# Five unread bfloat16 products of zeros ahead of each unit's and each chunk's work on TensorE, in a graph tensor product

## The chip, the cores and the metric

The kernel runs on one core of a Trainium2 chip. The metric is the device time of one execution in microseconds (us). Three runs of the kernel before took 8650.16, 8655.81 and 8651.81 us; the median is 8651.81 us.

## The reference, cut to what matters

There are N = 10000 nodes and E = 640000 edges; C = 64 channels and M = 4 components, so one node's features are 256 floats.

```python
def reference(x, src, dst, Y, edge_feat, w_rad, cg, w_mix):
    R = _silu(edge_feat @ w_rad)                              # (E, C)
    xs = x[src]                                               # (E, C, M)
    tp = jnp.einsum('eci,ef,ifo->eco', xs, Y, cg)             # (E, C, M)
    msg = R[:, :, None] * tp
    agg = _segment_sum(msg.reshape(-1, C * M), dst, N).reshape(N, C, M)
    return jnp.einsum('ncm,cd->ndm', agg, w_mix)
```

## The kernel before

The kernel sorts the edges by their destination on the chip, gathers each edge's source features from HBM, and adds up the messages of each bucket of 32 nodes with matrix products. The edges come in three parts (30, 35.5 and 34.5 per cent).

**First pass.** It takes chunks of 12 tiles of 128 edges and sorts them into 18 groups of nodes. `spread` (VectorE, DVE: X at L572) lays each edge's nine words into slots, `rows` (DVE L588; ScalarE, ACT: L594 and L595) makes a one-hot matrix oh, `move` (TensorE, PE: L602) multiplies the two into a PSUM tile pr, `evict` (ACT, L609) copies pr to rt, and `store` (GpSimd, POOL: L613) scatters rt to HBM with an indirect DMA. The tile pr has two buffers, X and oh three each; both passes share them.

**Second pass.** The same code (`route`) sorts a group into buckets, in chunks of 11 tiles, with one further product at L604 where a row is carried over from the chunk before. Ahead of the chunks, small tables are worked out on PE, DVE and ACT (L365 to L508; L365 is a series of bfloat16 products that count, L463 to L471 make destinations).

**Units.** `messages` handles one bucket of one part at a time: 939 units, 5 tiles in part 0 and 6 in the others. For unit k: `gather` (POOL, L893) issues one indirect DMA a tile, five units ahead, into one of 7 buffers xg. `turn` (PE, L911, two products) transposes the edge words into PSUM tile pre (two buffers), `turned` (ACT, L916) copies them out, `radial` (PE, L923 and L924) makes the radial factors in the same pre, `silu` (ACT, L927) applies the function. `spots` (DVE, L935 and L938) makes S. `products` (DVE, L945) multiplies the gathered features in place by the radial factors; it is the last reader of pre. `sums` (PE, L958) adds the unit up in one half of the PSUM tile G, with 10 or 12 float32 products that the profile shows as 20 or 24 records, and is the last reader of xg. `evict` takes that half of G out: by ACT in part 0 (L989), by DVE in parts 1 and 2 (L987), where the sum so far comes back from HBM. In part 2 `mix` (PE, L1006) multiplies four buckets' sums by the weights, and the result is stored.

**Order.** The first pass of part 0 runs alone (lag = 2). All the rest, called the main phase here, is one program with lag = 1, in which `groups` interleaves the units, the first pass of parts 1 and 2 and the second pass by counted steps. On PE, DVE and ACT the order of the main phase is the order of the code, and an engine executes it in order; POOL's and SP's order is chosen by the scheduler. One step of `messages` has four quarters:

```python
quarters = (((index, LI), (gather, LG), (fetch, 2), (turn, 2), (sums, 0), (silu, 1)), ((turned, 2), (spots, 1)),
            ((products, 1), (evict, -1), (pieces, 4)), ((radial, 2), (full, -1)))
```

The number beside a stage is the unit's distance, so in step k PE gets turn(k + 2) and then sums(k), and at the end radial(k + 2); DVE gets products(k + 1) and behind it evict(k - 1). turn(k + 2) takes the buffer of pre that products(k) read last, and sums(k) takes the half of G that evict(k - 2) read last.

After the last unit, two short loops treat rows that did not fit (L1123 to L1199).

Of the kernel before, what the change touches and what calls it, by code (L numbers as in the profile page):

```python
# [19 lines left out]
BF = mybir.dt.bfloat16  # L20
# [5 lines left out]
P = 128  # L26
# [10 lines left out]
LG = 5  # L37
LI = 8
HEAVY = 4
BIG = 16384.0  # L40
FAR = 2097152.0
KR = 108
# [31 lines left out]
class Kernel:  # L74
    def __init__(self, ctx, tc, x, src, dst, Y, ef, w_rad, cg, w_mix, out):
# [58 lines left out]
        self.tab = {}  # L134
        self.held, self.wanted, self.pos = None, False, None

    def bank(self, key):

        while self.held or self.wanted:
            yield "held"  # L140
        self.held = key


    def consts(self):
        nc, c = self.nc, self.cst

        def iota(name, pat, base=0, cm=0, at=c):
            t = at.tile([P] + [n for _, n in pat], F, name=name)
            nc.gpsimd.iota(t, pattern=pat, base=base, channel_multiplier=cm,
                           allow_small_or_imprecise_dtypes=True)  # L150
            return t

        self.zr = c.tile([16, max(self.p1.rw, self.p2.rw)], F, name="zr")
        nc.vector.memset(self.zr, 0.0)
        self.pid = iota("pid", [[0, 1]], cm=1)
        self.pid1 = iota("pid1", [[0, 1]], base=1, cm=1)
        self.i128 = iota("i128", [[1, P]])

        self.dv = self.ps.tile([P, 512], F, name="dv", tag="dv", bufs=1)
        self.v128 = self.dv[:, 0:P]  # L160
        nc.vector.tensor_copy(self.v128, self.i128)
        self.i32 = self.dv[:, 0:NB]
        self.eq = self.dv[:, P:P + UT * NB].rearrange("p (t n) -> p t n", n=NB)
        self.vmsk = self.dv[:, P + UT * NB:-B // 2]

        ib = self.ph.tile([P, B], BF, name="ib", bufs=1)
        nc.vector.tensor_copy(ib, self.i128[:, :B])
        nc.vector.tensor_copy(self.dv[:, -B // 2:].bitcast(I32), ib.bitcast(I32))
        self.vb = self.dv[:, -B // 2:].bitcast(BF)
        d = iota("dif", [[1, P]], cm=-1, at=self.ph)  # L170
        self.ident = c.tile([P, P], F, name="ident")
        nc.vector.tensor_scalar(self.ident, d, 0.0, None, op0=OP.is_equal)
        self.U = c.tile([P, P], F, name="U")
        nc.vector.tensor_scalar(self.U, d, 0.5, None, op0=OP.is_ge)

        self.U2 = c.tile([32, 2, 32], F, name="U2")
        self.id2 = c.tile([64, 32], BF, name="id2")
        for h in range(2):
            nc.vector.tensor_copy(self.U2[:, h, :], self.U[:32, :32])
            nc.vector.tensor_copy(self.id2[32 * h:32 * h + 32, :], self.ident[:32, :32])  # L180
        for p in (self.p1, self.p2):

            p.on = c.tile([64, B * (p.T + 1)], F, name="on" + p.key)
            nc.vector.memset(p.on, 1.0)
            nc.vector.memset(p.on.rearrange("p (b t) -> p b t", b=B)[:, :, 0:1], 0.0)
            p.cols = c.tile([64, B * (p.T + 1)], F, name="cols" + p.key)
            nc.vector.memset(p.cols, 0.0)
        self.Ub = c.tile([P, P], BF, name="Ub")
        nc.vector.tensor_copy(self.Ub, self.U)
        self.A = c.tile([P, P], BF, name="A")  # L190
        nc.vector.scalar_tensor_tensor(self.A, self.ident, BIG, self.U, op0=OP.mult, op1=OP.add)
        self.ones = c.tile([P, P], F, name="ones")
        nc.vector.memset(self.ones, 1.0)
        self.onesb = c.tile([P, P], BF, name="onesb")
        nc.vector.memset(self.onesb, 1.0)
        self.sel = c.tile([P, 2 * P], BF, name="sel")
        nc.vector.memset(self.sel, 0.0)
        nc.vector.memset(self.sel[:, P:P + 1], 1.0)
        nc.vector.memset(self.sel[:, P + 32:P + 33], 1.0)

        self.gb, self.gc = [], []
        for k in range(len(SPLIT)):
            gb = iota("gb%d" % k, [[self.p1.stride, B]], base=k * self.NG * self.p1.stride)
            gc = c.tile([P, B], F, name="gc%d" % k)
            nc.vector.memset(gc, 0.0)
            for g in range(self.NG):
                nc.vector.memset(gb[:, g:g + 1], float(self.gbase[k][g]))
                nc.vector.memset(gc[:, g:g + 1], float(self.gt[k][g] * P // self.p1.r))
            self.gb.append(gb)
            self.gc.append(gc)  # L210

        self.k1 = c.tile([1, B], F, name="k1")
        self.k2 = c.tile([1, self.NG * B], F, name="k2")
        self.kov = c.tile([1, 2], F, name="kov")
        nc.vector.memset(self.k2, 0.0)
        nc.vector.memset(self.kov, 0.0)
        self.bb = iota("bb", [[self.p2.stride, B]])
        self.bn = iota("bn", [[NB, B]])
        self.bc = c.tile([P, B], F, name="bc")
        nc.vector.memset(self.bc, float(self.p2.cap))  # L220
# [291 lines left out]
    def route(self, ps, quad, nt, table):  # L512
# [4 lines left out]
        nc, wk, tc, T, Q = self.nc, self.ph, self.tc, ps.T, 2  # L517
# [20 lines left out]
        def placed(q):  # L538
            m = min(Q * T, nt - q * Q * T)
            pp = PS.pop(q)  # L540
            pc = PP[q] = wk.tile([P, Q * T, B], F, name="pc", tag="pc" + ps.key, bufs=1)
            nc.scalar.activation(pc[:, :m, :], pp[:, :m, :], AF.Copy, bias=-BIG)  # L542

# [54 lines left out]
        def move(c):  # L598
            X, oh, m, on = XO.pop(c)
            pr = self.ps.tile([P, 512], F, name="pr", tag="route", bufs=2)  # L600
            for u in range(m):
                nc.tensor.matmul(pr[:, :ps.rw], oh[:, u, :], X[:, u, :], start=(u == 0), stop=(not on and u == m - 1))  # L602
            if on:
                nc.tensor.matmul(pr[:, :ps.rw], oh[:, m, :], RT[c - 1], start=False, stop=True)  # L604
            PR[c] = pr
# [17 lines left out]
        for k in range(-3 * Q, N + self.ls):  # L623
            if 0 <= k - lag - 1 < N:
                evict(k - lag - 1)
            if 0 <= k - lag < N:
                move(k - lag)
            if k % 2 and 0 <= k + 5 < N:

                while self.pos:  # L630
                    yield "held"
                self.pos = ps.key
                places((k + 5) // 2)
            if k % 2 == 0 and 0 <= k + 4 < N:
                placed((k + 4) // 2)
                self.pos = None
            if k % 2 == 0 and 0 <= k + 6 < N:
                prepare((k + 6) // 2)
            if 0 <= k < N:
                spread(k)  # L640
                yield "half"
                rows(k)
            if k % 2 and 0 <= k + 3 < N:
                slots((k + 3) // 2)
            if 0 <= k - self.ls < N:
                store(k - self.ls)

            yield (HEAVY - 2 if k < N else HEAVY) if 0 <= k < N + lag else 1

# [176 lines left out]
    def pass2_steps(self, k, g):  # L826
        nch = (self.gt[k][g] + self.p2.T - 1) // self.p2.T

        return 2 * (8 + self.ls) + HEAVY * nch + 20 * ((k, g) == self.segs[k * self.NG])


    def messages(self):

        nc, ph = self.nc, self.ph
        units = [((k, g), j, s) for k, g in self.segs for j in range(self.nb(g)) for s in range(len(SPLIT[k][1]))]
        MT = max(sum(u) for _, u in SPLIT)
        n = len(units)
# [172 lines left out]
        def mixed(k, po):  # L1010
# [5 lines left out]

        Gb, self.turns = self.ps.tile([P, 2, 2, NB, 4], F, name="G", tag="G", bufs=1), 0

        quarters = (((index, LI), (gather, LG), (fetch, 2), (turn, 2), (sums, 0), (silu, 1)), ((turned, 2), (spots, 1)),
                    ((products, 1), (evict, -1), (pieces, 4)), ((radial, 2), (full, -1)))  # L1020
        todo, po = [], None
        for k in range(-LI, n + 3):
# [16 lines left out]
    def groups(self):  # L1039
# [13 lines left out]
        for k in range(1, len(SPLIT)):  # L1053
            end = max(ends[k * NG - 2] - 8, at + 1)
            n = self.chunks(k)
            later.append((self.pass1(k, self.p1.NC), at, end, HEAVY * n + 20 * (n / (self.p1.NC - 2) + 2)))
            at = end
# [212 lines left out]
```

## Time and profile before

The profiled execution has a span of 8660.7 us from the first to the last instruction, 8.9 us above the median of the runs; no other time is shown for it.

| | busy us | instructions |
|---|---|---|
| PE, products | 6942.9 | 52148 |
| DVE | 7173.7 | 13741 |
| ACT | 4089.0 | 11736 |
| POOL | 6041.3 | 6308 |

The mean granted clock of TensorE over the span is 0.894 of full speed. A busy figure counts an engine's instructions alone; a product's record reaches from its start to its end, and since products follow one another in a pipeline their durations overlap. "X <- Y: a, b, c" in the view of waits says that X stood idle until Y released it, a us in total, b times, c us at the longest.

### The profile page before, as it was taken

How to read it: one execution, taken by the hardware profiler on the slowest of the kernel's cores; microseconds unless marked ns; L12 is line 12 of the kernel's file. 1: busy time of each engine (PE TensorE's matmuls, PEld its weight loads, DVE VectorE, ACT ScalarE, POOL GpSimd, SP SyncE). 2: the span in 40 equal slices, each digit the busy share in tenths (PEclk: the TensorE clock that was granted, in tenths of full speed). 3: DMA queues.
4: the chain of work that ended last, by engine and by line, in shares of the span. 5: the costliest groups of instructions: out<-in, count | busy, mean ns of one | idle time of the engine just before them, and what ended most of it. 6: DMA issues, size and time to landing. Idle time of an engine off the chain costs nothing. (4 is left out here: it accounts for less than half of the span.)

```text
span 8660.7 us, 149335 instructions
## 1 busy us (share of the span) xinstructions
PE 6942.9 (80%) x52148; PEld 6380.0 (74%) x52148; DVE 7173.7 (83%) x13741; ACT 4089.0 (47%) x11736; POOL 6041.3 (70%) x6308
## 2 busy tenths in 40 slices
PE   7978888888888778888888888866888878788875
PEld 6867777777777677777777777766777767777764
DVE  8989899889998788999989998877877768677754
ACT  6866555555556455454544554433333323333310
POOL 1236777667777767777777777777777777777775
PEclk9989999889999889999889899888998889888887
DMA  9313434334433434444444444444444444444442
GB/s 169 104 58 99 123 115 119 103 113 117 121 110 111 122 106 132 135 132 138 133 130 136 135 133 134 128 138 132 128 125 125 125 124 124 122 128 125 124 123 83
DMA packets 696289, 1056.64 MB, mean 122 GB/s; under 512 B 252018, under 2 KB 500226, under 8 KB 695536
## 3 DMA queue, kind: packets, MB, share of 16 engines
q0 software_dynamic: 286560, 746.71, 30.3%
q1 hardware_dynamic: 406384, 292.76, 12.2%
q8 instruction: 412, 6.75, 0.3%
q10 hardware_dynamic: 2592, 7.63, 0.3%
q14 instruction: 341, 2.79, 0.1%
HBM read 856.08 MB, written 207.12 MB: 123 GB/s over the span
## 5 line engine op out<-in xcount | busy, mean ns | idle before, releaser
L893 POOL DMA_INDIRECT xg<-in_x_dram,sidx x5321 | 5067.8, 952 | 1739.3 <-issue 1386.5
L602 PE MATMUL pr<-X,oh 128*128 128x126 f32 (+1 forms) x21112 | 2765.2, 289 | 395.7 <-ACT rt L609 215.6
L958 PE MATMUL G<-S,xg 128*128 128x128 f32 x21284 | 2953.1, 302 | 98.1 <-DVE Gp L987 62.8
L602 PEld LDWEIGHTS pr<-X,oh 128*128 128x128 f32 x21112 | 2638.2, 201 | 477.8 <-ACT rt L609 264.2
L958 PEld LDWEIGHTS G<-S,xg 128*128 128x128 f32 x21284 | 2803.5, 215 | 139.3 <-DVE Gp L987 86.2
L945 DVE TENSOR_TENSOR xg<-xg,pre 128x1536 f32<-128x1536 f32 (+1 forms) x939 | 1556.8, 1658 | 710.5 <-DMA xg<-in_x_dram,sidx 586.4
L594 ACT ACTIVATE sq<-i,rowf 128x128 f32<-128x128 f32 x5605 | 1735.7, 393 | 13.9 <-DVE rowf L559 13.4
L572 DVE TENSOR_TENSOR X<-dv,Wt 128x1512 f32<-128x1512 f32 (+4 forms) x958 | 1588.4, 1658 | 149.0 <-PE pr L602 94.8
L927 ACT ACTIVATE pre<-pre 128x384 f32<-128x384 f32 (+1 forms) x939 | 430.8, 459 | 1694.7 <-PE pre L924 1204.7
L595 ACT ACTIVATE oh<-sq,ones 128x768 f32<-128x768 f32 (+3 forms) x958 | 932.1, 973 | 32.9 <-issue 5.5
L938 DVE TENSOR_TENSOR S<-dv,pay 128x768 f32<-128x768 f32 (+1 forms) x939 | 857.4, 913 | 48.0 <-PE G L958 2.8
L613 POOL DMA_INDIRECT grp<-rt,idx x417 | 415.5, 996 | 585.9 <-ACT rt L609 240.1
L588 DVE TENSOR_TENSOR oh<-dv,rowf 128x640 f32<-128x640 f32 (+2 forms) x922 | 792.2, 864 | 0.5
L613 POOL DMA_INDIRECT bkt<-rt,idx x541 | 543.2, 1004 | 221.7 <-issue 125.8
L911 PE MATMUL pre<-identb,e 128*108 128x128 bf16 x1878 | 277.3, 231 | 523.4 <-DVE xg L945 513.6
L911 PEld LDWEIGHTS <-e 128*108 128x108 bf16 x1878 | 219.9, 133 | 604.5 <-issue 515.2
L916 ACT ACTIVATE sT<-pre 108x256 bf16<-108x256 f32 x939 | 353.5, 376 | 631.1 <-PE pre L911 628.4
L1006 PE MATMUL po<-wf,Gs 128*128 128x256 f32 (+2 forms) x1392 | 382.3, 436 | 150.7 <-DVE Gs L987 150.5
L542 ACT ACTIVATE pc<-pp 128x432 f32<-128x432 f32 (+3 forms) x506 | 243.7, 482 | 524.1 <-DVE pos L551 407.3
L1006 PEld LDWEIGHTS po<-wf,Gs 128*128 128x128 f32 (+2 forms) x1392 | 277.5, 205 | 238.3 <-DVE Gs L987 166.8
L609 ACT ACTIVATE rt<-pr 128x135 f32<-128x135 f32 (+1 forms) x958 | 258.8, 273 | 269.4 <-DMA bkt<-rt,idx 181.4
L923 PE MATMUL pre<-wr,sT 108*128 108x192 bf16 x939 | 240.2, 256 | 142.2 <-ACT sT L916 141.8
(240 smaller groups left out, 5309.3 us busy)
## 6 DMA issues: line engine op xcount, KB each, us to landing
xg<-in_x_dram,sidx POOLq DMA_INDIRECT x5321
sums<-Gp SPq DMA_DIRECT2D x626, 128.0 KB
old<-sums SPq DMA_DIRECT2D x626, 128.0 KB
bkt<-z SPq DMA_DIRECT2D x24, 994.5 KB
pay<-bkt SPq DMA_DIRECT2D x34, 486.0 KB
ys<-in_Y_dram SPq DMA_DIRECT2D x104, 96.0 KB
es<-in_edge_feat_dram SPq DMA_DIRECT2D x104, 96.0 KB
out_dram<-ot SPq DMA_DIRECT2D x69, 128.0 KB
```

The lines of the kernel that those rows point to most:

```text
L572: nc.vector.tensor_tensor(X[:, :m, :].rearrange("p t (s w) -> p t s w", w=W), msk.unsqueeze(3).to_broadcast([P, m, ps.r, W]), QD[c // Q][1 ...
L588: nc.vector.tensor_tensor(oh[:, :v, :], self.v128.unsqueeze(1).to_broadcast([P, v, P]), row[:, o:o + v].unsqueeze(2).to_broadcast([P, v, P ...
L594: nc.scalar.activation(sq[:, u, :], self.i128, AF.Square, bias=to, scale=-1.0)
L595: nc.scalar.activation(oh[:, v:v + len(at), :], sq[:, :len(at), :], AF.Relu, bias=self.ones[:, 0:1], scale=-2.0)
L602: nc.tensor.matmul(pr[:, :ps.rw], oh[:, u, :], X[:, u, :], start=(u == 0), stop=(not on and u == m - 1))
L613: st = nc.gpsimd.indirect_dma_start(out=ps.dst, out_offset=bass.IndirectOffsetOnAxis(ap=idx[:, i:i + 1], axis=0), in_=RT.pop(c), in_offset ...
L893: nc.gpsimd.indirect_dma_start(out=xg[:, t, :], out_offset=None, in_=self.x, in_offset=bass.IndirectOffsetOnAxis(ap=si[:, u:u + 1], axis=0))
L911: nc.tensor.matmul(pre[:KR, 256 + 128 * h:384 + 128 * h], e[:, 36 * t:36 * t + KR], self.identb, start=True, stop=True)
L938: nc.vector.tensor_tensor(S[:, :ut], self.eq[:, :ut].unsqueeze(3).to_broadcast([P, ut, NB, 4]), pb[:, :, 1:5].unsqueeze(2).to_broadcast([P ...
L945: nc.vector.tensor_tensor(V, V, R.unsqueeze(3).to_broadcast([P, ut, 64, 4]), op=OP.mult)
L958: nc.tensor.matmul(G[:, h].rearrange("p n f -> p (n f)"), V[:, t, 32 * h:32 * h + 32, :].rearrange("p c i -> p (c i)"), S[:, t].rearrange( ...
L1006: nc.tensor.matmul(po[:nn, :256], Gs[:, h, f].rearrange("p b n -> p (b n)")[:, :nn], self.wf[:, h, f, :], start=(h + f == 0), stop=(h + f ...
```

## The change

A helper `keep` issues n products of a bfloat16 tile of zeros zb: 128 columns of it are the weights and 256 the moving operand. The main phase calls it with n = 5 at two places. In `move`, ahead of a chunk's products, the result goes to columns 256 to 511 of the chunk's own pr tile, of which the chunk uses at most 135 of the first columns. In `messages`, a new stage `busy` ahead of `turn` writes to the half of G that this step's `sums` is about to start afresh. Nothing reads the results of either.

```diff
+KEEP = 5
@@ Kernel
+    def keep(self, out, n):
+
+        for _ in range(n):
+            self.nc.tensor.matmul(out, self.zb[:, :P], self.zb, start=True, stop=True, skip_group_check=True)
@@ consts
+        self.zb = c.tile([P, 256], BF, name="zb")
+        nc.vector.memset(self.zb, 0.0)
@@ move
             pr = self.ps.tile([P, 512], F, name="pr", tag="route", bufs=2)
+            if self.lag == 1:
+                self.keep(pr[:, 256:], KEEP)
             for u in range(m):
@@ messages
-        quarters = (((index, LI), (gather, LG), (fetch, 2), (turn, 2), (sums, 0), (silu, 1)), ((turned, 2), (spots, 1)),
+        def busy(k):
+            self.keep(Gb[:, self.turns % 2].rearrange("p h n f -> p (h n f)"), KEEP)
+
+        quarters = (((index, LI), (gather, LG), (fetch, 2), (busy, 0), (turn, 2), (sums, 0), (silu, 1)), ((turned, 2), (spots, 1)),
```

## The prediction

> **What bounds the kernel now.** I read the page first, then the busy time by stage, then the waits of each stage. The stages are A (800 to 3200 us) and B (3200 to 5600), in which units, first-pass and second-pass chunks are mixed, and C (5600 to 8450), in which the first pass is over; these three rows give length, then busy us and count of PE, weight loads, DVE, ACT and POOL, then the granted clock.
>
> ```profile
> span 8660.7 us, 149335 instructions
> ...
> 800.00:3200.00 2400.00, 1955.75 (x15302) 1819.66 (x15301) 2147.47 (x4165) 1341.98 (x3928) 1717.31 (x1787) 0.91 0.40 114
> 3200.00:5600.00 2400.00, 1968.16 (x15328) 1834.56 (x15327) 2170.00 (x3996) 1205.60 (x3428) 1815.90 (x1891) 0.91 0.46 133
> 5600.00:8450.00 2850.00, 2262.54 (x16132) 2063.49 (x16131) 2071.41 (x3745) 972.67 (x2686) 2161.71 (x2259) 0.88 0.44 126
> ```
>
> POOL's 70% misleads. Between two gathers stands a pause of 0.3 us that nothing explains but "issue" (1240 such pauses in stage A, below, of 0.3 at the longest), so a POOL instruction takes 1717.31 / 1787 = 0.96 us and the pause. With 0.3 us on each instruction POOL is taken for 1717 + 1787 x 0.3 = 2253 of 2400 us in A, 1816 + 567 = 2383 of 2400 in B, and 2162 + 678 = 2840 of 2850 in C. In B and C POOL is full; in A it stands idle for some 147 us. DVE stands at 89% and 90% in A and B and at 73% in C; PE at 81%, 82% and 79%.
>
> The waits of stage A (of POOL, of PE, of DVE), then the longest of DVE and one of POOL in B, and the longest of DVE in C:
>
> ```profile
> POOL xg L893 <- issue: 377.8, 1240, 0.3
> POOL xg L893 <- PE G L958: 81.0, 42, 7.7
> ...
> POOL xg L893 <- PE stp L451: 15.3, 3, 13.2
> POOL xg L893 <- PE pre L924: 14.5, 16, 4.6
> POOL xg L893 <- PE pre L911: 13.1, 18, 4.1
> ```
> ```profile
> PE pre L911 <- DVE xg L945: 147.1, 73, 6.8
> PE pr L602 <- ACT rt L609: 112.9, 78, 4.3
> PE ddp L469 <- DVE to L463: 47.0, 15, 8.1
> PE pr L602 <- DVE oh L588: 25.8, 21, 4.9
> ```
> ```profile
> DVE X L572 <- PE pr L602: 48.7, 23, 5.4
> DVE sts L471 <- PE ddp L469: 25.8, 13, 5.5
> ...
> DVE xg L945 <- ACT pre L927: 13.1, 12, 2.5
> ```
> ```profile
> DVE Gp L987 <- PE G L958: 34.4, 20, 5.8
> DVE X L572 <- PE pr L602: 33.9, 16, 6.6
> ```
> ```profile
> POOL xg L893 <- PE G L958: 10.1, 12, 3.5
> ```
> ```profile
> DVE xg L945 <- DMA xg<-in_x_dram,sidx: 507.2, 135, 6.8
> ```
>
> In A, POOL waits for PE to free gather buffers: 81.0 + 15.3 + 14.5 + 13.1 = 123.9 us, or 100 without the 79 pauses of 0.3. There the loop of DVE, PE and ACT sets the pace, with DVE its busiest member. In B neither side holds the other: POOL waits 10.1 us for sums, and DVE's two longest waits, 34.4 and 33.9 us, are for PE, so that what it waits for gathered data is less; both go at almost the same pace. In C DVE waits 507 us for data: POOL sets the pace alone, and the others have room. A gain is thus capped at about 100 + 10 us, and a loss in A, and in most of B, goes into the time.
>
> **What the change adds.** 939 groups of five on G and 834 on pr (958 chunks less the 124 that part 0 has under lag = 2), 8865 products, each with a weight load, and one memset. Nothing is removed; the waits move. For a product's price the nearest rows are the bfloat16 counting products in a row, at full clock and, in C, at half:
>
> ```profile
> 4456.11 1.08 PE L365 MATMUL cnt<-D,sel 128*64 128x198 bf16 x11
> ```
> ```profile
> 6535.56 1.88 PE L365 MATMUL cnt<-D,sel 128*64 128x198 bf16 x11
> ```
>
> Eleven take 1.08 us; leaving some 0.19 for the last one to run out, a step is about 0.089, and (1.88 - 0.23) / 10 = 0.165 at half clock. The loads are hidden in that. For 256 columns in place of 198 this is 0.115 and 0.213, so five cost 0.57 us at full and 1.07 at half clock. Lower bound of a group: nothing, where PE would have idled; upper bound 1.07.
>
> The clock matters because PE loses it after its own waits:
>
> ```profile
> 4003.07 2.90 PE L958 MATMUL G<-S,xg 128*128 128x128 f32 x24
> ...
> 4008.10 1.74 DVE L945 TENSOR_TENSOR xg<-xg,pre 128x1536 f32<-128x1536 f32 x1
> ...
> 4009.76 0.41 DVE L987 TENSOR_TENSOR Gp<-old,G 128x256 f32<-128x256 f32 x1
> ...
> 4012.23 1.06 PE L469 MATMUL ddp<-bd,ones 11*128 11x209 f32 x2 [3.10 <-DVE to L463]
> ...
> 4013.73 5.40 PE L958 MATMUL G<-S,xg 128*128 128x128 f32 x24
> ```
> ```profile
> 4003.00:4006.00 3.00, 3.00 (x27) 2.86 (x27) 2.86 (x7) 2.85 (x10) 2.14 (x3) 1.00 0.33 89
> 4013.70:4018.70 5.00, 5.00 (x26) 5.00 (x25) 4.69 (x15) 4.91 (x15) 3.78 (x5) 0.50 0.26 73
> ```
>
> A unit's sums take 2.90 us at clock 1.00 and 5.40 at 0.50, after PE had stood for 3.10 us. A mean of 0.91 between 1.00 and 0.50 means half clock for 18% of A and B.
>
> Do the groups fill PE's waits? Mostly not. `busy` writes the half of G that evict(k - 2) reads, and in parts 1 and 2 DVE executes that evict right behind products(k): in the rows above L945 starts at 4008.10 for 1.74 us and L987 ends at 4010.17. So where turn waits for products (73 times in A) the group starts only after the wait, and turn comes later by 0.41 us of evict and 0.57 of zeros; queued behind it on PE are sums, the next chunk's products and radial, and for these wait POOL (xg), DVE (X) and ACT (silu). In `move` the group waits for the same release of pr as the chunk did (ACT rt, 112.9 us in A), and only the waits for oh (25.8 us) can be filled. What the groups do shorten is PE's next wait, since PE arrives there later; that is where the clock can gain.
>
> [...]
>
> Counts for the load are these rows of A and B, the turns first (two a unit), then the chunks:
>
> ```profile
> 800.00:3200.00 2400.00, 86.93 (x588) 67.94 (x588) 0.91 0.40 114
> 3200.00:5600.00 2400.00, 78.88 (x534) 61.33 (x534) 0.91 0.46 133
> ```
> ```profile
> 800.00:3200.00 2400.00, 81.19 (x303) 0.91 0.40 114
> 3200.00:5600.00 2400.00, 78.74 (x296) 0.91 0.46 133
> ```
>
> A has 294 + 303 = 597 groups, 340 us at full clock, against 444 us in which PE is idle; B has 267 + 296 = 563, 321 us against 432. The load fits, barely: 96% and 95% with nothing won back.
>
> **The sum.** (1) DVE, the busiest of the loop, waits for PE 23 + 13 times in A, 12 times for silu, which hangs on PE's radial, and 20 + 16 times in B: 84 times. I estimate that two groups lie between PE's own last wait and such a release (a unit's and a chunk's): 84 x 2 x 0.57 = 96 us. Bounds: 0, if PE's earlier idle time takes them all; 84 x 4 x 1.07 = 360. (2) Credit for the clock: a DVE wait on PE is likelier where PE is slow, so I take twice the 18%, 2.5 us each (5.40 less 2.90), and let half of it vanish: 84 x 0.36 x 2.5 / 2 = 38 us. Bounds: 0, and all the waits of DVE on PE, 48.7 + 25.8 + 13.1 + 34.4 + 33.9 = 156. (3) Releases that are now just in time become waits: unknown, 0 to another 96; I take 25, because PE is up to 1 us later in most steps and the listed waits average about 2 us. (4) In B the two paces are apart by a little, and POOL takes up some of a loss: I estimate 15 us, of 0 to 17 (2400 - 2383). (5) C: at most 1773 - 597 - 563 = 613 groups, 349 us, lie in 2850 - 2263 = 587 us of PE's idle time while POOL sets the pace: nothing; without that cover, up to 349. The memset is nothing beside 8600 us. After the last gather one group is on the way to the end: 1 us. The changed order of a few stores among POOL's gathers: each moves by one instruction, nothing.
>
> 96 - 38 + 25 - 15 + 1 = +69 us. The profiled execution would be 8730 us; it lies 8.9 us above the median of the runs, so I forecast 8721 us, 0.8% slower.
>
> **Rivals.** Faster: the zeros carry PE over its waits, the half-clock stretches go, and with them POOL's waits in A. For it: 18% at half clock, and a burst late by 2.5 us weighs more than 0.57. Against it: the groups stand behind the waits they should fill. At the cap of 110 us the time is 8542; at half of it 8597. [...]
>
> PE becomes the bound: if the clock does not recover, groups cost 18% more: A needs 1956 + 340 x 1.18 = 2357 us of PE, B 1968 + 379 = 2347. If half of today's waits remain as well (222 and 216), the stages take 2579 and 2563: +342, 8994 us. It decides once PE's waits shrink by less than the groups add. For it: the waits on DVE are forced from outside. Against it: later arrival shortens them one for one.
>
> No change that shows: groups and credit cancel, or the loop's room covers both: 8652 us. A difference below 0.2%, 17 us, is no change for this kernel's measurement.
>
> **How the numbers follow.** Forecast (slower by 17 to about 200 us) 0.46; PE the bound 0.14; no change 0.12; faster 0.28. The forecast's own range is 8670 to 8850. The range for 8 in 10 goes down to 8580, past half the cap, and up to 8890, where PE is the bound for part of A and B. Faster 0.28, same 0.12, slower 0.60.
>
> **What would show it.** Right: POOL's waits on PE in A grow beyond 123.9 us and appear in B; DVE's waits on X and Gp grow; PE's waits before L911 shrink; the clock in A and B rises a little, to about 0.94, and C keeps its length. Wrong: POOL's waits in A shrink and the clock goes to 0.97 or more (faster), or PE stands above 95% busy with DVE's waits doubled (bound). If C gets longer, my reading of POOL is wrong.

## The result, and the profile after

The changed kernel takes 8748.21 us (median of 4 runs, 8746.84 to 8751.17) against 8650.99 us for the kernel before on the same chip (4 runs). The ratio is 1.011, 95% interval 1.0096 to 1.0124: 97 us slower, where 69 were forecast.

The page of the kernel after, and its busy time in the three stages (length, then busy us and count of PE, weight loads, DVE, ACT, POOL, then clock, DMA share and GB/s):

```profile
span 8746.2 us, 166012 instructions
...
PE 7524.1 (86%) x61013; PEld 6908.6 (79%) x61013; DVE 7183.5 (82%) x13742; ACT 4108.6 (47%) x11736; POOL 6042.4 (69%) x6308
```
```profile
800.00:3200.00 2400.00, 2127.90 (x17897) 1969.55 (x17895) 2098.52 (x4064) 1315.25 (x3830) 1676.54 (x1744) 0.95 0.39 112
3200.00:5600.00 2400.00, 2135.71 (x17927) 1988.34 (x17926) 2158.75 (x4000) 1207.32 (x3428) 1784.36 (x1857) 0.95 0.45 130
5600.00:8450.00 2850.00, 2423.17 (x19031) 2217.69 (x19031) 2093.84 (x3766) 1003.18 (x2757) 2161.06 (x2260) 0.93 0.44 127
```

POOL's count is the measure of progress, since POOL paces the kernel wherever it does not wait. In B before, full, it executed 1891 instructions in 2400 us, 1.27 us each. In the same 2400 us it now gets through 1744 in place of 1787 in A, and 1857 in place of 1891 in B. That is 43 and 34 fewer, 77 x 1.27 = 98 us: the whole loss. In C it executes 2260 (2259 before): nothing is lost there, though PE carries 160 us more. The clock rose from 0.91 to 0.95 in A and B, and from 0.88 to 0.93 in C.

The longest waits of stage A after, of POOL, of DVE and of PE (total, times, longest), and then those of POOL and of DVE in B:

```profile
POOL xg L903 <- issue: 365.1, 1192, 2.1
POOL xg L903 <- PE G L968: 112.6, 58, 6.3
POOL xg L903 <- PE pre L934: 36.8, 26, 5.7
...
POOL xg L903 <- PE stp L459: 16.3, 2, 13.6
```
```profile
DVE X L580 <- PE pr L612: 73.7, 31, 6.6
DVE xg L955 <- ACT pre L937: 46.6, 29, 3.3
DVE sts L479 <- PE ddp L477: 31.6, 12, 6.0
```
```profile
PE pr L141 <- ACT rt L619: 111.6, 80, 4.3
PE pre L921 <- DVE xg L955: 37.8, 26, 5.2
PE G L141 <- ACT Gp L999: 21.7, 43, 4.1
```
```profile
POOL xg L903 <- PE G L968: 36.6, 25, 7.6
```
```profile
DVE Gp L997 <- PE G L968: 57.4, 45, 6.1
DVE X L580 <- PE pr L612: 56.2, 24, 7.6
...
DVE Gp L997 <- DMA sums<-Gp: 5.5, 2, 2.9
```

POOL's waits on PE grew in both stages: in A to 112.6 + 36.8 + 16.3 = 165.7 us, and in B, for sums, from 10.1 to 36.6.

Five rows of DVE's waits on PE, three of A (of which ACT's L937 hangs on PE's radial) and two of B, went from 48.7 + 25.8 + 13.1 to 73.7 + 31.6 + 46.6 us in A, and from 34.4 + 33.9 to 57.4 + 56.2 in B: from 155.9 to 265.5 us, and in number from 84 to 72 + 69 = 141. The mean over all five hardly moved (1.86 and 1.88 us), but it mixes the rows. In the three rows of A and in X of B the mean wait grew, by 0.2 to 0.65 us; only the waits for Gp in B became shorter (1.72 to 1.28) while their number went from 20 to 45. If each row's old count is taken at its change of mean, and its change of count at the new mean, about 15 of the 110 us are longer waits and about 94 are more waits; this split is an estimate, since single waits can't be matched between the two traces. Most of the growth is thus releases that come too late only now.

These rows are not the whole of DVE's idle time. Two others of B got shorter; before they were:

```profile
DVE Gp L987 <- issue: 31.6, 4, 9.4
DVE Gp L987 <- DMA sums<-Gp: 25.0, 5, 8.3
```

After, the second has 5.5 us and the first is gone. By its busy time DVE idled 49 us more in A and 11 more in B, 60 us together and not 110.

The groups of PE, by line (count, busy us, mean ns of one, idle before it and what ended that):

```profile
L612 PE MATMUL pr<-X,oh 128*128 128x126 f32 (+1 forms) x21112 | 2669.8, 283 | 95.4 <-DVE oh L596 69.4
L968 PE MATMUL G<-S,xg 128*128 128x128 f32 x21284 | 2709.3, 286 | 0.0
...
L141 PE MATMUL G<-zb 128*128 128x256 bf16 x4695 | 699.8, 282 | 335.2 <-DVE Gp L997 174.7
...
L141 PE MATMUL pr<-zb 128*128 128x256 bf16 x4170 | 608.4, 278 | 195.9 <-ACT rt L619 194.5
```

PE's own work got cheaper as the mean granted clock over the span went from 0.894 to 0.940: sums 2953.1 to 2709.3 us (302 to 286 ns each), the chunks' products 2765.2 to 2669.8 (289 to 283), together 339 us won back. The groups of zeros are busy for 699.8 + 608.4 = 1308 us, which is more than they cost, because the end of a group overlaps the work behind it: in the timeline below a series of 0.71 us holds up the next product by 0.54, and one of 1.27 us by 1.06. At the first share they cost some 1308 x 0.54 / 0.71 = 1000 us (an estimate). PE's whole busy time rose by 7524.1 - 6942.9 = 581 us. The idle time that stood before the sums and the chunks' products stands before the zeros now, which wait for the evict of G (174.7 us of it for Gp of part 1) and for rt (194.5).

In the timeline of the kernel after a group is seen at both clocks (start, length of the series, and how PE idled before it):

```profile
2001.20 0.71 PE L141 MATMUL pr<-zb 128*128 128x256 bf16 x5
2001.74 2.71 PE L612 MATMUL pr<-X,oh 128*128 128x135 f32 x22
...
2007.73 0.55 PE L477 MATMUL ddp<-bd,ones 9*128 9x171 f32 x2 [2.47 <-DVE to L471]
...
2008.42 1.27 PE L141 MATMUL pr<-zb 128*128 128x256 bf16 x5
2009.48 0.85 PE L612 MATMUL pr<-X,oh 128*128 128x126 f32 x3
```

From the first of five to the chunk's first product it is 0.54 us, with a granted clock of 1.00 from 2001.20 to 2004.40, and 1.06 us after PE had idled 2.47 us, with a clock of 0.50 from 2008.42 to 2009.70.

### The profile page after: what moved, and what is told of

It reads as the page before. It is cut to its first block, busy times and chain, and to the rows that moved or that the text cites. A ratio compares the mean times of both kernels' runs of the same rounds, so it can differ in the third digit from the quotient of the medians.

```text
span 8746.2 us, 166012 instructions
## 1 busy us (share of the span) xinstructions
PE 7524.1 (86%) x61013; PEld 6908.6 (79%) x61013; DVE 7183.5 (82%) x13742; ACT 4108.6 (47%) x11736; POOL 6042.4 (69%) x6308
## 5 line engine op out<-in xcount | busy, mean ns | idle before, releaser
L612 PE MATMUL pr<-X,oh 128*128 128x126 f32 (+1 forms) x21112 | 2669.8, 283 | 95.4 <-DVE oh L596 69.4
L968 PE MATMUL G<-S,xg 128*128 128x128 f32 x21284 | 2709.3, 286 | 0.0
L612 PEld LDWEIGHTS pr<-X,oh 128*128 128x128 f32 x21112 | 2569.8, 196 | 140.2 <-DVE oh L596 82.5
L968 PEld LDWEIGHTS G<-S,xg 128*128 128x128 f32 x21284 | 2583.1, 200 | 0.1
L141 PEld LDWEIGHTS <-zb 128*128 128x128 bf16 x8865 | 854.0, 99 | 737.3 <-issue 624.3
L937 ACT ACTIVATE pre<-pre 128x384 f32<-128x384 f32 (+1 forms) x939 | 430.4, 458 | 1810.0 <-PE pre L934 1338.3
L141 PE MATMUL G<-zb 128*128 128x256 bf16 x4695 | 699.8, 282 | 335.2 <-DVE Gp L997 174.7
L141 PE MATMUL pr<-zb 128*128 128x256 bf16 x4170 | 608.4, 278 | 195.9 <-ACT rt L619 194.5
L945 DVE TENSOR_TENSOR dv<-dv,dlc 128x192 f32<-128x192 f32 (+1 forms) x939 | 330.8, 352 | 16.4
```

The lines of the kernel that those rows point to most:

```text
L141: self.nc.tensor.matmul(out, self.zb[:, :P], self.zb, start=True, stop=True, skip_group_check=True)
L968: nc.tensor.matmul(G[:, h].rearrange("p n f -> p (n f)"), V[:, t, 32 * h:32 * h + 32, :].rearrange("p c i -> p (c i)"), S[:, t].rearrange( ...
```

## The experiments

Each ratio is to the kernel before on the same chip, with its 95% interval. The runs above e4 in the table ran on a chip where the kernel before takes 8652.99 us (17 runs, 8648 to 8666), the others on one where it takes 8659.25 us (25 runs, 8652 to 8671).

| run | what it has | median us | ratio |
|---|---|---|---|
| e1_units_only | five zeros, units | 8674.52 | 1.0023 (1.0012 to 1.0034) |
| e2_chunks_only | five zeros, chunks | 8704.67 | 1.0055 (1.0038 to 1.0072) |
| e3_wait_without_load | one product of 16 columns, both places | 8658.91 | 1.0004 (0.9995 to 1.0014) |
| e7_ten | ten zeros, both places | 9077.79 | 1.0492 (1.0475 to 1.0510) |
| e4_units_behind_turn | five zeros, units, behind turn | 8676.97 | 1.0023 (1.0013 to 1.0032) |
| e8_units_no_wait | five zeros, units, in a persistent pr tile | 8712.64 | 1.0061 (1.0044 to 1.0078) |
| e6_part0_only | five zeros, units of part 0 | 8678.58 | 1.0022 (1.0012 to 1.0032) |
| e5_part2_only | five zeros, units of part 2 | 8662.78 | 1.0003 (0.9994 to 1.0013) |

**One kind at a time.** Two theories stood against each other: that the zeros cost as load on PE, and that they cost through the wait that turn got with them.

```diff
 e1: without
-            if self.lag == 1:
-                self.keep(pr[:, 256:], KEEP)
 e2: without
-(busy, 0),
```

> The five zeros ahead of the units' turns stay, those ahead of the chunks' products go. Load theory (each group lengthens PE's work where DVE and POOL wait for PE, in stages A and B, and both kinds cost alike): the share of the groups, 939 of 1773, of the 97 us: about 8700 us, 8690 to 8715. Wait theory (the loss is that turn now stands behind the evict of G, and the zeros themselves are covered): nearly the whole loss, 8735 to 8750.

> The five zeros ahead of the chunks' products stay, those ahead of the turns go. Load theory: 834 of 1773 groups, about 8697 us, 8685 to 8710. Wait theory: the chunk's zeros wait for the release of pr that the chunk waited for already, so nothing is lost: 8650 to 8660.

The chunks' zeros, which brought no new wait, cost more than twice as much as the units' zeros, which did. The wait theory fails on both. The load theory holds for the chunks' zeros (8704.67 us of 8685 to 8710) and is too high for the units' zeros (8674.52 us, under its 8690). It missed in that the two kinds do not cost alike, and the two losses do not add up to the whole: 0.23 + 0.55 is 0.78%, the change cost 1.1%. POOL's counts suggest where the difference is. These are stages A and B of e1, then of e2:

```profile
800.00:3200.00 2400.00, 2053.81 (x16738) 1902.63 (x16735) 2142.15 (x4141) 1343.22 (x3917) 1708.26 (x1776) 0.94 0.39 114
3200.00:5600.00 2400.00, 2053.46 (x16640) 1915.11 (x16641) 2168.73 (x3996) 1207.70 (x3421) 1810.74 (x1884) 0.93 0.45 132
```
```profile
800.00:3200.00 2400.00, 2028.04 (x16533) 1883.02 (x16532) 2108.67 (x4079) 1315.23 (x3847) 1686.94 (x1754) 0.93 0.39 113
3200.00:5600.00 2400.00, 2069.39 (x16814) 1921.78 (x16813) 2173.03 (x4019) 1217.07 (x3463) 1804.92 (x1881) 0.94 0.45 131
```

In A, e1 loses 11 POOL instructions and e2 33; together 44, and the change loses 43: there the losses add. In B they lose 7 and 10, together 17, and the change loses 34. It looks as if B has room for most of the one kind or the other, and not for both. The counts are of one execution each, and executions of one kernel differ: in the profiled one of e4 below (8659.37 us, the fastest of ten), which has the units' zeros too, POOL executes 1787 and 1890 instructions in A and B, as good as nothing less than before. So this is a reading, and not shown.

**The wait without the load.**

```diff
-KEEP = 5
+KEEP = 1
-            self.nc.tensor.matmul(out, self.zb[:, :P], self.zb, ...)
+            self.nc.tensor.matmul(out[:, :16], self.zb[:, :P], self.zb[:, :16], ...)
```

> One product of 16 columns in place of five of 256, at both places: the waits and the order of the changed kernel with under a tenth of its load. Load theory: 8650 to 8670 us, granted clock back at about 0.89. Wait theory: 8720 to 8750 us.

No difference can be told, with a granted clock of 0.904 over the span (0.899 before on this chip): the new wait and the new order alone cost at most 0.14%, so it takes the load for the 1.1%. e4, below, shows for the units' zeros that the load costs the same where it brings no new wait.

**Twice the load.**

```diff
-KEEP = 5
+KEEP = 10
```

> Ten zeros in place of five. Load theory: PE would be busy for some 2128 + 340 = 2468 of 2400 us in stage A, so it becomes the bound there and in B: the loss grows more than twofold, 8880 to 9000 us. Rival (the warmer clock pays the second five): 8750 to 8830 us with the clock at 0.97 or more.

The second five cost 328 us where the first five cost 97; 9077.79 us lies above even the 8880 to 9000 that the load theory gave, and far above the rival, though the clock (0.968 over the span) is about what the rival asked (0.97). Stages A and B of e7, and DVE's longest waits in its stage A:

```profile
800.00:3200.00 2400.00, 2233.39 (x19377) 2064.31 (x19376) 1944.72 (x3735) 1223.20 (x3553) 1568.62 (x1632) 0.98 0.36 105
3200.00:5600.00 2400.00, 2246.88 (x19442) 2081.73 (x19441) 2040.87 (x3832) 1146.21 (x3257) 1669.03 (x1737) 0.98 0.42 121
```
```profile
DVE X L580 <- PE pr L612: 158.2, 55, 9.0
DVE xg L955 <- ACT pre L937: 94.7, 43, 5.7
```

PE is busy for 93 and 94% and has taken DVE's place as the busiest of the loop: DVE falls from 2147 to 1945 us in A. The clock reaches 0.98 of full speed, so at most 0.02 is left to win. This is the prediction's rival in which PE becomes the bound, or near to it. It has no sharp beginning: with five zeros PE's busy time in A (2127.90 us) is already above DVE's (2098.52).

**The place of the units' zeros.**

```diff
 e4: without the chunks' zeros, and
-(busy, 0), (turn, 2), (sums, 0)
+(turn, 2), (busy, 0), (sums, 0)
 e8: without the chunks' zeros, and
+        self.prb, self.free = self.ps.tile([P, 2, 512], F, name="prb", tag="route", bufs=1), [0, 1]
     (move takes the two halves of prb in turn as its pr, evict gives them back)
-            self.keep(Gb[:, self.turns % 2].rearrange("p h n f -> p (h n f)"), KEEP)
+            self.keep(self.prb[:, 0, 256:], KEEP)
```

> Units' zeros only, put between turn and sums: sums waited for the evict of G before, so no wait is new, and turn is as early as before. Load theory: as with the units' zeros ahead of turn, at most 15 us less, since turn's 0.41 us behind the evict is gone. Wait theory: the loss goes, 8650 to 8660 us.

> Units' zeros only, ahead of turn, written to unused columns of a persistent tile that nothing waits for; they run in the idle time in which PE waits for products. Load theory: where PE waits (about 70 of 290 units in A) the group is free, elsewhere it still costs: two thirds of the loss of the units' zeros, 8675 to 8700 us. Rival (zeros in the gap keep the clock up and win time): below 8640 us.

Behind turn they cost what they cost ahead of it, as the load theory had it; the wait theory fails again. e8 went against its expectation: 0.61%, and not less than 0.23%. But its edit does not do what it was for. Over the span of e8, and then of the kernel before:

```profile
PE prb L141 <- ACT rt L620: 24.4, 20, 8.4
```
```profile
ACT rt L620 <- PE prb L612: 299.5, 142, 8.1
ACT rt L620 <- PE prb L614: 147.1, 52, 6.3
ACT rt L620 <- PE prb L141: 91.2, 38, 6.0
```
```profile
ACT rt L609 <- PE pr L602: 77.6, 57, 4.2
ACT rt L609 <- PE pr L604: 9.1, 7, 2.2
```

The zeros do wait, for ACT's copy of pr, and that copy waits 537.8 us for PE where it waited 86.7: 91.2 of it for the zeros, the rest for chunks' products. The persistent tile has tied zeros, chunks and copies to one another, so e8 says nothing on zeros without a wait. Whether zeros inside PE's waits are dearer stays open.

**By stage.**

```diff
+            if units[k][0][0] != 0:     # e6; != 2 in e5; both without the chunks' zeros
+                return
```

> Units' zeros in part 0 alone (313 units, stage A, up to about 3300 us). Load theory: A took 54 of the 96 us that POOL's waits grew by, the units' zeros half of it: plus 20 to 35 us on the kernel before, 8671 to 8686. If stage A has room: 8651.

> Units' zeros in part 2 alone (313 units, stage C). POOL full there: 8648 to 8660 us, though PE carries 313 groups more. If the reading of POOL is wrong and PE's load counts everywhere: plus 20 to 35 us, 8671 to 8686.

Part 0 alone costs 0.22%, as much as all units' zeros; part 2 alone nothing that can be told. So the units' zeros cost in stage A, and PE's load in C is free while POOL paces it. Part 1 alone was not run; what is left for it is 0.23 - 0.22 - 0.03%, nothing that can be told, but each of the three ratios is uncertain by 0.1%.

**A chip that does not compare.** A last set ran on a chip where the kernel before took 10443.86 us (9 runs).

```diff
 e9: the chunks' keep moved behind the loop over the chunk's products, no units' zeros
 e8c: e8 with
+KEEP = 0
 e10:
+KEEP = 2
 e11: both kinds; in move, and busy returns unless the unit is of part 1
+            if self.lag == 1 and self.stage == 1:
```

> Chunks' zeros only, put behind the chunk's own products: same load as the chunks' zeros ahead, but they wait for nothing, so they run where PE would otherwise begin to wait. Filling theory (a group costs little where it runs inside a wait of PE, and much where it stands behind the wait, as ahead of the chunk's products behind the release of pr): the loss of 0.55% falls to that of the units' zeros or less, 8650 to 8680 us. Plain load theory (place does not matter): 8690 to 8710 us.

> The persistent pr tile of the run without waits, with no zeros at all: a control. If that tile costs nothing, 8650 to 8660 us, and then zeros in the gap are dearer than zeros behind it, against the filling theory; if the loss of 0.61% was the tile's own, 8690 to 8710 us.

> Two zeros in place of five, at both places. Load theory with room (POOL full in stage B takes up small losses): clearly less than two fifths of the 97 us, 8655 to 8685. Rival (a fixed cost a group): 8700 us or more. Rival (a few zeros win clock): below 8640 us.

> Both kinds, only while the units are of part 1 (stage B). Units' zeros alone were free there, chunks' zeros nearly so. Room theory: B has room for one kind and not for both, so about the half of the 97 us that fell in B remains or less, as A now hands over no backlog: 8665 to 8700 us. If the losses only add up: 8650 to 8662 us.

Measured: e9 10647.59 us, ratio 1.0195 (1.0181 to 1.0209); e8c 10531.24, 1.0082 (1.0068 to 1.0096); e10 10574.53, 1.0126 (1.0110 to 1.0141); e11 10575.48, 1.0128 (1.0112 to 1.0143). The expectations were made for a kernel of 8650 us, and the losses found on the other chips were not measured on this one, so none of the four is decided. e8c has no zeros at all and loses 0.8%: at least there the tile of e8 is not free, in line with e8's own waits above. Two zeros (e10) lose there as much as five did elsewhere. On the face of it that speaks for the rival of a fixed cost a group; without the change itself on that chip it can't be told from the chip's own slowness. No run was faster than the kernel before, and nothing seen here points to a version that would be.

## Why the prediction was right

**What bounds the kernel.** Right in all three stages. POOL paces C, and the load there was free (e5; 2259 and 2260 instructions). In A POOL waits for PE, and its loss of pace is in the time. POOL pauses 0.3 us between instructions and so is full at 76% busy (B); with that its counts could be turned into time, 98 of 97 us. On B the prediction overlooked that DVE also waited 31.6 + 25.0 us ahead of Gp for something other than PE.

**The price of a group.** Forecast 0.57 and 1.07 us from the counting products; 0.54 and 1.06 in the timeline. The 0.19 and 0.23 us set aside for the last product's end stood on no row that the prediction shows; the shortest products of its two counting series took 0.190 and 0.222 us, and the step came out: 0.54 / 5 = 0.108 us for 0.115, and 1.06 / 5 = 0.212 for 0.213.

**Terms 1 to 3, the loop.** Their sum was 96 - 38 + 25 = 83 us; the five rows of DVE's waits grew by 110. The sum was near and its parts were not, so that it came near is in part luck. Term 1 let each existing wait grow by 1.14 us, and the credit took some of that off: 58 us together. By the split above, longer waits are only about 15. Term 3, releases that become late only now, was put at 25 us, without a row for it, and is the term that was mis-sized: about 94 by the same split. How much of term 1 the clock paid for was not separated.

**Term 4, POOL's room in B.** 15 us were estimated, and no run measures it: the 110 us of five rows are not a sum that POOL could have cut to 97, since other waits of DVE shrank. e1 and e2 suggest what the term did not say: the room is used up by the first kind of zeros, so the second costs more.

**Do the groups fill PE's waits?** "Mostly not" was wrong for the units in part 0. The prediction read the order from rows at 4003 to 4019 us, in part 1, and laid it on the 73 waits of stage A, whose units are of part 0. There ACT, not DVE, takes G out, and it is mostly done early, so that zeros can run while PE waits for products: the wait ahead of turn in A fell from 147.1 to 37.8 us, and only 21.7 stand ahead of the zeros. In part 1 it was right: the zeros wait for DVE's evict (116.7 us, 70 times in B). For the chunks it was right too: the wait for rt, 112.9 us, stands ahead of the zeros, 111.6. This may be why the chunks' zeros cost more in A (33 POOL instructions against 11); e9 was to test it and could not, so it is not shown.

**The clock.** 0.94 forecast for A and B, 0.95 measured. The group at 2008.42 us stayed at 0.50 throughout its 1.06 us, but with zeros all over the loop the mean over the span rose from 0.894 to 0.940, and 339 us of PE's time came back. With the same waits and order and less load (e3) it was 0.904. Whether the zeros kept the clock from being lost or won it back sooner was not separated.

**The rivals.** The faster one failed though its mechanism worked: the clock went up (0.894 to 0.940 over the span), and PE's whole busy time went up by 581 us all the same. PE as the bound, or near to it, is what ten zeros bring (93% and 94% busy in A and B). That the new order and the new waits cost the time by themselves is excluded by e3.

## What to carry to other kernels

Zeros that raise TensorE's granted clock, here from 0.894 to 0.940 over the span, pay only if they cost less time than they win back; count both, here some 1000 us of zeros (an estimate) against 339, and check the balance by PE's whole busy time, here 581 us more. Do not take an engine's idle share for room when another engine's order hangs on it. PE idled 18% of stage A in many short waits and was not free for 14% more work (an estimate, 597 groups x 0.57 us in 2400): with five zeros PE was 89% busy in A and B, DVE's late releases in the five rows had grown from 84 to 141, and the loss was 97 us; with ten, PE was 93% and 94% busy and the loss 425. Read the pace from the instruction count of the engine that is full in equal windows; it turns a loss into places.

## What the runs showed of the hardware that was not expected

The mean granted clock over the span was higher with more products of zeros, though nothing reads their results: 0.894 before and 0.940 with five; on the chip of e7, 0.899 before, 0.904 with one of 16 columns (e3) and 0.968 with ten (e7).

One chip ran the kernel before in 10443.86 us, where the first took 8650.99. Of e10 on that chip, the page's groups of gathers and of sums, PE's two longest waits over the span, two waits of POOL and ACT, and a chunk's series in the timeline:

```profile
L903 POOL DMA_INDIRECT xg<-in_x_dram,sidx x5321 | 5074.0, 954 | 3107.4 <-issue 1373.2
L968 PE MATMUL G<-S,xg 128*128 128x128 f32 x21284 | 3176.5, 309 | 381.5 <-issue 367.4
```
```profile
PE pr L612 <- issue: 380.4, 584, 1.9
PE G L968 <- issue: 367.4, 526, 1.9
```
```profile
ACT pre L937 <- remote: 951.8, 152, 17.2
...
POOL xg L903 <- remote: 604.6, 316, 2.8
```
```profile
4021.36 0.98 PE L612 MATMUL pr<-X,oh 128*128 128x135 f32 x7
4024.03 1.91 PE L612 MATMUL pr<-X,oh 128*128 128x135 f32 x15 [1.69 <-issue]
```

A gather takes 954 ns there and 952 in the kernel before on its own chip, so POOL's work is no slower; PE's sums take 309 ns where they took 302, at a lower granted clock (0.855 over the span, 0.894 before). But PE stops in the middle of a chunk's products, for 1.69 us in the row shown, where it waits for nothing that the profile shows; the two rows count over a thousand such waits; the kernel after on its own chip has no idle time at all before its sums. ACT and POOL stand idle there until a release that the profile puts down to "remote", that is, to no instruction that it recorded; the traces of the kernels before and after have no such row. What holds the engines back on that chip is not known.
